# Ending the deferred output projection eleven granules earlier in a streamed-weight attention kernel

## The chip, the cores and the metric

The kernel runs on one core of one Trainium2 chip. The metric is the device time of one execution in microseconds, as the median of several executions. The kernel before takes 1866.62 us (median of 3 runs, 1864.03 to 1872.82).

## The reference

A sequence of 2048 rows of width 1024 is normalised (`xn`) and goes through two branches whose results are added to `x`.

```python
# branch A: 64 segments of 32 rows, one after the other
for s in range(n_seg):
    xs = x[:, s*32:(s+1)*32, :]
    h = concatenate([mem, xs], axis=1)         # 8 memory rows + 32 rows
    q = einsum('btd,dhe->bhte', h, Wq)         # 32 heads of 128
    k = einsum('btd,dhe->bhte', h, Wk)
    v = einsum('btd,dhe->bhte', h, Wv)
    p = softmax(where(mask, q @ k.T * scale, -1e9))
    o = einsum('bhte,hed->btd', p @ v, Wo)
    mem = o[:, :8, :]                          # memory of the next segment
    outs.append(o[:, 8:, :])
# branch B: the 2 best of 2048 rows by x @ w_r go through a gated MLP (1024 -> 3584 -> 1024)
return x + A(xn) + B(xn)
```

The segments depend on one another only through the 8 memory rows. Of the 40 rows of a segment, the first 24 rows of its input together with the 8 memory rows (32 rows) are what the next segment needs. The last 8 input rows of a segment, called the *left* rows here, are not needed by the recurrence. Four segments form a *group*, and the left rows of a group (4 x 8 = 32 rows) go through the weights together, one group ahead for q, k and v and after the group for the output projection.

## The kernel before, in words

**Steps, phases and granules.** There are 64 steps, one a segment; a step `s` is `j = s % 4` of its group. The weights are cut into 64 granules of 128 x 2048 bf16 (512 KB). Granules 0 to 47 are six phases of eight: q first half, k first half, q second half, k second half, v first half, v second half. Granules 48 to 63 are the sixteen pieces of the output projection. A step walks through all 64 in order: `(p, kc)` is granule `8*p + kc`, and `(6, w)` is granule `48 + w`. In each granule TensorE (PE) makes 4 matmuls of 32 x 512 side by side in the array for the 32 main rows (L817), or 8 of 32 x 256 in the output projection (L586).

**Resident and streamed weights.** 44 granules stay on the chip. The other 20 are fetched again in each step (19 after the first step, since granule 6 is kept in PSUM, and half of granule 25 is too) from a scratch copy in HBM (`wsc`) into 5 slots (`g`). The fetches are issued on SyncE's queue (SP, L366), each as soon as the slot that it will fill has been released by the last PE instruction that reads it. Before granule 25 is used, VectorE (DVE) copies its kept half from PSUM into its slot (L393, hooks (2,1) and (2,2)).

**Work hung into the order.** Small pieces of work are hung behind granules: `hook(p, kc, fn)` runs `fn` in the program's order behind granule `8*p + kc`. The engines execute their instructions in that order, each its own list. What matters here:

- behind phase 1 ScalarE (ACT) casts the k sums to `XB` (L836); at (2,3) PE transposes them (L649) and DVE copies them to `KT` (L664), with a small ACT copy of the left rows' k (L662);
- at (2,6) PE makes the scores of the first half, `scores(0)` (L672, L674), into the PSUM tile `BS`; they need the whole of `KT`. DVE then masks and shifts them (L681 to L687);
- at (3,4) ACT takes the exponent (L691) and DVE normalises and transposes (L696 to L720, `soften(0)`);
- at (4,6) PE makes the scores of the second half, `scores(1)`, into the same `BS`, so it waits until `soften(0)` has read it;
- in steps with `j = 0` POOL (GpSimd) loads the next group's left x (L333 into `BX`, hook (1,1)); in every step it loads the next segment's x at (2,4) (L281).

**Passes of the left rows.** `PASSES` says behind which granule of which `j` each left pass is made. A pass is 4 matmuls of 32 x 512 (L579 for q, k, v; L598 for the output projection, `project_left`, into the PSUM tile `WL`). The 16 passes of unit `o` (granules 48 to 63) begin in the step `j = 3` of a group and end in the step `j = 0` that follows. `COPIES` says where a unit's sums are copied out. For `o` this is `copy_unit`: two ACT copies of 64 x 256 (L616) into `LF`, two DVE adds (L619) into `LF`, one POOL add (L620) of `LF` and the scaled left x `OL`, and four DMAs on POOL's queue (L624). `OL` is loaded at the end of the step `j = 3` (L333) and scaled by `sum_left` on DVE (five small instructions, L275 to L347).

The lists at the top of the program (`PASSES`, `COPIES`) and the calls of `hook` set the order by hand; no planner changes it.

Of the kernel before, what the change touches and what calls it, by code (L numbers as in the profile page):

```python
# [43 lines left out]
}  # L44

COPIES = {"q0": (1, 1, 0, "scalar"), "q1": (1, 5, 7, "vector"), "k0": (2, 2, 0, "scalar"), "k1": (2, 5, 7, "vector"),
          "v0": (3, 4, 7, "scalar"), "v1": (3, 5, 7, "scalar"), "o": (0, 3, 3, "vector")}


@with_exitstack  # L50
def kernel(
# [221 lines left out]
    def two_rows(m, tag):  # L273
        t = one.tile([P, 4], F32, tag=tag, name="RI")
        nc.vector.tensor_copy(out=t[:, 0:1], in_=m[:, 0:1])  # L275
        nc.vector.reciprocal(out=t[:, 1:2], in_=m[:, 1:2])
        return t
# [63 lines left out]
    def sum_left(t, G):  # L341

        mr = two_rows(ML[:, G, :], "ri")
        nc.vector.tensor_scalar(out=mr[:, 0:1], in0=mr[:, 0:1], scalar1=mr[:, 1:2], scalar2=-1.0,
                                op0=ALU.mult, op1=ALU.mult)
        nc.vector.tensor_scalar(out=mr[:, 1:2], in0=mr[:, 1:2], scalar1=1.0, scalar2=None, op0=ALU.add)
        nc.vector.tensor_scalar(out=t[:, :], in0=t[:, :], scalar1=mr[:, 1:2], scalar2=mr[:, 0:1],  # L347
                                op0=ALU.mult, op1=ALU.add)
# [241 lines left out]
    xl_of, otl_of = [None], [None]  # L590
# [41 lines left out]
    for s in range(NSEG):  # L632
        G, j = divmod(s, 4)
# [9 lines left out]
        def hook(p, kc, fn):  # L643
            hooks.setdefault((p, kc), []).append(fn)
# [140 lines left out]
                held.pop(g)  # L785
                after(s, g)
        if j == 0 and s > 0:
            hook(2, 3, lambda: sum_left(xl_of[0], G - 1))
        hook(*((1, 0) if s > 0 else (2, 3)), clear_pl)
        if s > 0:  # L790
            hook(0, 0, lambda: bring_back(3, nc.scalar.copy))
# [222 lines left out]
```

## Time and profile before

| | before |
|---|---|
| median of the runs | 1866.62 us |
| the profiled execution, time | 1871.21 us |
| its span, first to last instruction | 1869.1 us |
| mean granted TensorE clock | 0.957 |
| PE busy | 1568.8 us (84%) |
| DVE / ACT / POOL busy | 896.9 / 683.6 / 457.1 us |
| moved by DMA | 712.27 MB, mean 381 GB/s |

Times in the profile are microseconds from the first instruction. PE is a matmul, PEld a weight load (which overlaps matmuls), SPq and POOLq are engines in their role of issuing DMAs. A row of the timeline is: start, duration, engine, line, operation, what it writes and reads, how many instructions are merged in it, and in brackets how long the engine sat idle before it and what ended that. `A <- B: t, n, m` in the list of waits means that instructions A waited `t` us in total for B, `n` times, `m` us at the longest.

### The profile page before, as it was taken

To read this page: it belongs to the slowest core of one execution; us is meant where nothing else is said; L and a number is where in the kernel's file an instruction comes from. 1 tells how busy PE (TensorE), PEld (TensorE's weight loads), DVE (VectorE), ACT (ScalarE), POOL (GpSimd) and SP (SyncE) were. 2 spreads that over 40 slices of the span, in tenths; PEclk is the share of its full clock that TensorE was granted. 3 is DMA by queue.
4 is the path that set the end of the run, shared out by engine and by line. 5 is a ranking of instruction groups with operands and counts; after the bars stand their busy time and mean duration, and the time that the engine had idled before them with its cause. 6 is when DMAs were issued, how large, how long until landed. Compare 5 with 4: busy or idle time off the path is not lost.

```text
span 1869.1 us, 80529 instructions
## 1 busy us (share of the span) xinstructions
PE 1568.8 (84%) x34978; PEld 847.9 (45%) x34978; DVE 896.9 (48%) x2950; ACT 683.6 (37%) x1933; POOL 457.1 (24%) x898
## 2 busy tenths in 40 slices
PE   3458998898998988888899988988889988988764
PEld 1124444444444444444444444444445544444433
DVE  6725544554455444544554455544544455445430
ACT  1113433444343433434344334434334343433320
POOL 3111322213231322223132322323132221312220
PEclk8669999999999999999999999999999999999995
DMA  9999999999999999999999999999999999999998
GB/s 370 406 355 373 388 386 380 393 382 387 394 385 392 366 383 391 359 380 385 388 375 388 389 384 387 373 396 374 378 369 396 394 382 383 378 377 352 384 402 338
DMA packets 230322, 712.27 MB, mean 381 GB/s; under 512 B 39040, under 2 KB 52912, under 8 KB 229968
## 3 DMA queue, kind: packets, MB, share of 16 engines
q1 hardware_dynamic: 192592, 671.18, 93.0%
q0 software_dynamic: 28736, 28.08, 4.7%
q10 hardware_dynamic: 8640, 7.87, 1.2%
q8 instruction: 274, 4.49, 0.9%
q14 instruction: 80, 0.66, 0.1%
HBM read 694.32 MB, written 22.29 MB: 383 GB/s over the span
## 4 chain that ended last, share of the span: by engine, by line
DMA 61%; PE 32%; DVE 4%; issue 1%; ACT 1%; SPq 0%; ACTq 0%; DVEq 0%
DMA g<-wsc 54%; PE PSm L817 17%; PE WO L586 4%; PE PSl L579 4%; PE BT L649 2%; DMA XP<-in_A_x_dram 2%; PE WL L598 1%; DMA MW<-in_B_w_gate_dram 1%; DVE XR L256 1%; DMA MW<-in_B_w_up_dram 1%; DMA g<-in_A_Wq_dram 1%; DMA wres<-in_A_Wo_dram 1%; DMA g<-in_A_Wo_dram 1%; DMA MW<-in_B_w_down_dram 1%; DMA g<-in_B_w_down_dram 1%
## 5 line engine op out<-in xcount | busy, mean ns | idle before, releaser
L817 PE MATMUL PSm<-wres,ST 128*32 128x512 bf16 x8448 | 700.5, 383 | 6.5 <-DMA wres<-in_A_Wv_dram 3.5
L817 PEld LDWEIGHTS <-ST 128*32 128x32 bf16 x12288 | 323.6, 96 | 412.7 <-issue 168.2
L817 PE MATMUL PSm<-g,ST 128*32 128x512 bf16 x3588 | 360.0, 386 | 97.7 <-DMA g<-wsc 76.3
L586 PEld LDWEIGHTS <-OT 128*32 128x32 bf16 x8192 | 217.6, 97 | 166.6 <-issue 141.0
L836 ACT CAST XB<-PSm 128x512 bf16<-128x512 f32 x256 | 150.7, 589 | 283.9 <-PE PSm L817 280.8
L586 PE MATMUL WO<-wres,OT 128*32 128x256 bf16 x5632 | 237.6, 278 | 12.3 <-DMA wres<-in_A_Wo_dram 8.0
L495 POOL DMA_DIRECT2D LX<-ql_d x63 | 35.4, 562 | 814.0 <-PE WO L586 423.2
L586 PE MATMUL WO<-g,OT 128*32 128x256 bf16 x2560 | 133.3, 281 | 84.1 <-DMA g<-wsc 72.6
L579 PE MATMUL PSl<-wres,STL 128*32 128x512 bf16 x2112 | 184.5, 390 | 0.4 <-issue 0.4
L887 POOL DMA_DIRECT2D out_dram<-X x256 | 130.2, 515 | 211.9 <-DVE X L885 169.4
L664 DVE COPY KT<-BT 128x512 bf16<-128x512 bf16 x112 | 45.9, 410 | 278.7 <-issue 121.8
L281 POOL DMA_DIRECT2D X<-in_A_x_dram x256 | 130.1, 515 | 179.6 <-PE PSm L817 88.8
L389 ACT COPY BK<-KEPT 128x512 bf16<-128x512 bf16 x126 | 74.3, 590 | 131.2 <-PE WO L586 99.8
L657 ACT COPY QT<-BT 128x512 bf16<-128x512 bf16 x128 | 75.0, 586 | 127.1 <-PE BT L502 78.1
L649 PEld LDWEIGHTS <-XB 128*128 128x128 bf16 x1024 | 58.6, 98 | 117.1 <-ACT XB L836 75.2
L885 DVE TENSOR_TENSOR X<-WO,X 128x256 bf16<-128x256 f32 x64 | 27.2, 425 | 172.3 <-PE WO L586 172.3
L649 PE MATMUL BT<-IDENT,XB 128*128 128x128 bf16 x1024 | 102.2, 223 | 8.2 <-ACT XB L836 6.7
L579 PEld LDWEIGHTS <-STL 128*32 128x32 bf16 x3072 | 84.0, 98 | 53.0 <-issue 8.5
L846 ACT CAST VM<-PSm 128x512 bf16<-128x512 f32 x128 | 76.5, 598 | 83.3 <-PE PSm L817 82.8
L736 PEld LDWEIGHTS <-VM 32*128 32x128 bf16 x2048 | 65.1, 91 | 83.7 <-issue 72.7
L393 DVE COPY g<-KEPT 128x512 bf16<-128x512 bf16 x126 | 47.6, 420 | 101.7 <-PE PSm L817 51.5
L681 DVE TENSOR_TENSOR BS<-BS,CT 128x96 f32<-128x96 f32 (+1 forms) x256 | 59.1, 231 | 72.8 <-PE BS L674 68.3
(175 smaller groups left out, 2371.9 us busy)
## 6 DMA issues: line engine op xcount, KB each, us to landing
g<-wsc SPq DMA_DIRECT2D x1134, 512.0 KB, 6.0
g<-wsc SPq DMA_DIRECT2D x63, 256.0 KB, 5.7
LX<-ql_d POOLq DMA_DIRECT2D x63, 128.0 KB, 5.6
ql_d<-XBl ACTq DMA_DIRECT2D x60, 128.0 KB, 5.8
MW<-in_B_w_gate_dram SPq DMA_DIRECT2D x16, 448.0 KB, 9.5
MW<-in_B_w_up_dram SPq DMA_DIRECT2D x16, 448.0 KB, 9.1
wres<-in_A_Wk_dram SPq DMA_DIRECT2D x12, 512.0 KB, 11.9
MW<-in_B_w_down_dram SPq DMA_DIRECT2D x12, 512.0 KB, 10.1
```

The source lines that it names most:

```text
L281: nc.gpsimd.dma_start(out=X[s % 2][32 * g:32 * g + XM, :], in_=x2[s * SEG:s * SEG + XM, 256 * g:256 * (g + 1)])
L389: copy(out=back[c][:, :], in_=KEPT_COLS[KEPT_WHOLE][c])
L579: nc.tensor.matmul(PSl[32 * jq:32 * jq + 32, :], lhsT=STL[:, g % KC, :], rhs=part(Gv, jq), start=first_, stop=last_, tile_position=(0, 32 ...
L586: nc.tensor.matmul(PS[32 * g:32 * g + 32, 0:256], lhsT=lhs(h), rhs=Gv[:, D * hs + 256 * g:D * hs + 256 * (g + 1)], start=(first and hs == ...
L649: nc.tensor.transpose(out=PTq[:, il, :, :].rearrange("p j r -> p (j r)"), in_=XB[:, il * P:(il + 1) * P], identity=IDENT[:, :])
L657: nc.scalar.copy(out=QT[half][:, :, :], in_=pv)
L681: nc.vector.tensor_tensor(out=S4, in0=S4, in1=m, op=ALU.add)
L736: nc.tensor.matmul(o, lhsT=VM[half][q0:q0 + 32, il * P:(il + 1) * P], rhs=PTm[q0:q0 + 32, il, 0:NK], start=True, stop=False, tile_position ...
L817: nc.tensor.matmul(PSm[32 * jq:32 * jq + 32, :], lhsT=ST[:, kc, :], rhs=part(Gv, jq), start=(kc == 0), stop=(kc == KC - 1), tile_position= ...
L836: nc.scalar.copy(out=XB[:, :], in_=PSm[:, :])
L846: nc.scalar.copy(out=VM[half][:, :], in_=PSm[:, :])
L887: nc.gpsimd.dma_start(out=out2[s * SEG:s * SEG + XM, 256 * g:256 * (g + 1)], in_=OB[32 * g:32 * g + XM, :])
```

## The change

Three things move, and only in steps with `j = 0` (steps 4, 8, ... 60: fifteen steps):

1. The last six passes of unit `o`. Before, they stood behind granules 7, 11, 15, 19, 22 and 26 of the step. Now they stand behind granules 4, 7, 10, 12, 14 and 16.
2. `copy_unit("o")`, from (3,3) to (2,1): before, behind granule 27; now behind granule 17, one granule after the last pass. All its instructions move, on ACT, DVE, POOL and POOL's DMA queue.
3. `sum_left`, from (2,3) to (1,4).

The number of instructions is the same on every engine, and SyncE's list is unchanged.

```diff
 PASSES["o"]:
-          (3, 8, 0): [52, 54], (0, 0, 7): [55], (0, 1, 3): [57], (0, 1, 7): [58], (0, 2, 3): [60], (0, 2, 6): [61],
-          (0, 3, 2): [63]},
+          (3, 8, 0): [52, 54], (0, 0, 4): [55], (0, 0, 7): [57], (0, 1, 2): [58], (0, 1, 4): [60], (0, 1, 6): [61],
+          (0, 2, 0): [63]},
...
 COPIES:
-          "v0": (3, 4, 7, "scalar"), "v1": (3, 5, 7, "scalar"), "o": (0, 3, 3, "vector")}
+          "v0": (3, 4, 7, "scalar"), "v1": (3, 5, 7, "scalar"), "o": (0, 2, 1, "vector")}
...
         if j == 0 and s > 0:
-            hook(2, 3, lambda: sum_left(xl_of[0], G - 1))
+            hook(1, 4, lambda: sum_left(xl_of[0], G - 1))
```

**DVE, from the start of a `j = 0` step to `soften(0)`.** `L885` and `L324` belong to the step's start, `L347` is the last of `sum_left`, `L619` are the adds of `copy_unit`, `L393` fills granule 25's kept half, `L664` makes `KT`, and `L681` is the first instruction after `scores(0)`. Before:

```order
L389 COPY BK<-KEPT_193 128x512
L393 COPY g<-KEPT_195 128x512 x2
L664 COPY KT<-BT 128x16x32
L275 COPY RI<-BS 128x1
...
L347 TENSOR_SCALAR OL<-OL,RI 128x256
L681 TENSOR_TENSOR BS<-BS,CT 128x4x24
...
L687 TENSOR_TENSOR BS<-BS,NM 128x320
L619 TENSOR_TENSOR LF<-WL,LF 64x256 x2
L696 TENSOR_REDUCE DN<-BS 128x8
```

Now:

```order
L389 COPY BK<-KEPT_193 128x512
L275 COPY RI<-BS 128x1
...
L347 TENSOR_SCALAR OL<-OL,RI 128x256
L619 TENSOR_TENSOR LF<-WL,LF 64x256 x2
L393 COPY g<-KEPT_195 128x512 x2
L664 COPY KT<-BT 128x16x32
L681 TENSOR_TENSOR BS<-BS,CT 128x4x24
...
L687 TENSOR_TENSOR BS<-BS,NM 128x320
L696 TENSOR_REDUCE DN<-BS 128x8
```

(What is left out, the middle of `sum_left` and of the masking, stands in the same order in both.) The two adds stood between `scores(0)` and `soften(0)`; they now stand ahead of the two copies L393 and of `KT`.

**ACT, behind phase 0's `QKL`.** `L836` is the cast behind each phase, `L616` are the copies of `copy_unit`, `L691` is the exponent of the first half.

```order
 L506 COPY QKL<-BT 128x512
 L836 CAST XB<-PSm 128x512
-L662 COPY KT<-QKL 128x16x8
-L836 CAST XB<-PSm 128x512
-L657 COPY QT<-BT 128x512
 L616 COPY LF<-WL 64x256 x2
+L662 COPY KT<-QKL 128x16x8
+L836 CAST XB<-PSm 128x512
+L657 COPY QT<-BT 128x512
 L691 ACTIVATE BS<-BS 128x320
```

The two copies stood just ahead of the exponent; they now follow the cast of phase 1, ahead of the small `KT` copy.

**POOL, in the same step.** `L620` adds `LF` and `OL`, `L624` stores, `L281` loads the next segment's x.

```order
 L763 MEMSET BX 128x256
 L333 DMA BX<-in_A_x_dram 32x1x256 x4
-L281 DMA X_131<-in_A_x_dram 24x256 x4
-L620 TENSOR_TENSOR OL<-LF,OL 128x256
-L624 DMA out_dram<-OL 4x8x256 x4
+L620 TENSOR_TENSOR OL<-LF,OL 128x256
+L624 DMA out_dram<-OL 4x8x256 x4
+L281 DMA X_131<-in_A_x_dram 24x256 x4
```

The add and the stores stood behind the load of x; they now stand ahead of it.

## The prediction

> **What bounds the kernel now.** I read the page first, then the waits and one line's view of the stream, then the timeline of one `j = 0` step.
>
> ```profile
> span 1869.1 us, 80529 instructions
> ...
> DMA  9999999999999999999999999999999999999998
> ...
> HBM read 694.32 MB, written 22.29 MB: 383 GB/s over the span
> ...
> DMA 61%; PE 32%; DVE 4%; issue 1%; ACT 1%; SPq 0%; ACTq 0%; DVEq 0%
> ```
>
> The DMA engines are busy in every slice, and 61% of the chain of waits is transfer. PE is the next link, 32%: each fetch needs a slot that PE has released. So the stream of weights sets the pace, and PE matters where it releases late.
>
> ```profile
> L885 DVE TENSOR_TENSOR X<-WO,X x64: 424/425/427, 129.5 to 1810.4; 128x256 bf16<-128x256 f32 x64
> ...
> g<-wsc SPq DMA_DIRECT2D x1134, 512.0 KB, 6.0
> ...
> DMA to landing us min/median/max: 3.3/6.0/10.3
> ...
> SPq L366 <- PE PSm L817: 422.9, 640, 2.7
> SPq L366 <- DMA g<-wsc: 396.5, 740, 2.5
> ...
> PE PSm L817 <- DMA g<-wsc: 76.3, 154, 2.5
> PE WO L586 <- DMA g<-wsc: 72.6, 150, 2.0
> ```
>
> L885 ends each step: 63 steps in 1680.9 us are 26.7 us a step. A fetch of 512 KB (0.524 MB) at 383 GB/s is 1.37 us of transfer, but lands 6.0 us after its issue in the median and 3.3 us at best. So 2.7 us (about two granules) is waiting behind others: that is the reserve which keeps the DMA engines fed. PE waits for data 76.3 + 72.6 us in all, 2.4 us a step, and SP waits for PE about as long as for transfers.
>
> The step below (`j = 0`, from 528.7 to 554.8) is where the change acts; first PE from the end of phase 1 to `scores(0)`:
>
> ```profile
> 532.46 0.40 PE L817 MATMUL PSm<-g,ST 128*32 128x512 bf16 x4 [0.19 <-DMA g<-wsc]
> ...
> 534.89 0.40 PE L598 MATMUL WL<-wres,OTL 128*32 128x512 bf16 x4
> 535.10 0.40 PE L817 MATMUL PSm<-wres,ST 128*32 128x512 bf16 x4
> 535.52 0.40 PE L817 MATMUL PSm<-g,ST 128*32 128x512 bf16 x4
> ...
> 536.50 0.40 PE L649 MATMUL BT<-IDENT,XB 128*128 128x128 bf16 x4
> 536.83 0.40 PE L817 MATMUL PSm<-wres,ST 128*32 128x512 bf16 x4
> 537.06 0.39 PE L817 MATMUL PSm<-g,ST 128*32 128x512 bf16 x4
> ...
> 537.71 0.19 PE L672 MATMUL BS<-KT,QT 128*32 128x40 bf16 x4
> ```
>
> A pass or a granule takes PE 0.21 us (534.89 to 535.10), the four transposes 0.33. Next, what ACT and DVE do around it, and POOL's rows:
>
> ```profile
> 534.62 0.59 ACT L506 COPY QKL<-BT 128x512 bf16<-128x512 bf16 x1
> 535.12 0.59 ACT L836 CAST XB<-PSm 128x512 bf16<-128x512 f32 x1
> 540.43 0.74 ACT L616 COPY LF<-WL 64x256 f32<-64x256 f32 x2
> 541.09 0.42 ACT L691 ACTIVATE BS<-BS 128x320 f32<-128x320 f32 x1
> ...
> 531.46 0.76 DVE L393 COPY g<-KEPT 128x512 bf16<-128x512 bf16 x2 [1.26 <-DMA g<-wsc]
> 536.99 0.42 DVE L664 COPY KT<-BT 128x512 bf16<-128x512 bf16 x1 [4.78 <-issue]
> 539.65 0.50 DVE L687 TENSOR_TENSOR BS<-BS,NM 128x320 f32<-128x320 f32 x1
> 541.21 0.86 DVE L619 TENSOR_TENSOR LF<-WL,LF 64x256 f32<-64x256 f32 x2 [1.06 <-ACT LF L616]
> 542.10 0.49 DVE L696 TENSOR_REDUCE DN<-BS 128x8 f32<-128x320 f32 x1
> 543.21 0.29 DVE L715 TENSOR_TENSOR BX<-BS,DN 128x64 bf16<-128x64 f32 x1
> 543.55 0.11 PEld L672 LDWEIGHTS <-QT 128*32 128x32 bf16 x3 [0.50 <-DVE BX L715]
> ...
> 542.16 0.67 POOL L620 TENSOR_TENSOR OL<-LF,OL 128x256 bf16<-128x256 f32 x1 [4.65 <-DVE LF L619]
> 543.12 2.44 POOL L624 DMA_DIRECT2D out_dram<-OL  x4 [0.29 <-POOL OL L620]
> ...
> 549.69 0.34 DVE L292 TENSOR_SCALAR XN<-X,RI 128x256 bf16<-128x256 bf16 x1
> ```
>
> Two things to see. DVE had L393 done at 532.2 and then stood idle 4.78 us, free for `KT` as soon as PE had transposed. And `scores(1)` (543.55) waits for `soften(0)`, which the LF copies and adds hold up. The first is lost by the change, the second is won.
>
> **The change, part by part.** All work is kept; what counts is order, in fifteen steps.
>
> *Passes earlier.* Five passes instead of two now stand ahead of the end of phase 1: 3 x 0.21 = 0.64 us later. In this step PE waits for granule 9 (0.19, and the pipeline's own gap beside it), which takes up one pass: +0.43. So `XB`, at 535.12, starts at 535.55. From step to step this is between 0.2 and 0.65.
>
> *The new wait.* The last pass follows one granule later; PE is done with it at 535.55 + 0.43 = 535.98. ACT's next instruction can start 0.50 after `XB` (534.62 to 535.12): LF copies 536.05 to 536.79. DVE's adds 0.04 behind (541.17 to 541.21), 0.86: to 537.69. Then, queued behind them, L393's 0.76 to 538.47 and `KT`'s 0.42 to 538.89. PE's scores come 0.30 behind `KT` (537.41 to 537.71): **539.19 instead of 537.71, 1.5 us later**. Without the wait PE would be there at 535.98 + six granules (1.29) + 0.33 = 537.60. So PE stands idle 1.6 us at (2,6), once in each of the fifteen steps. Behind it on PE wait granules 23, 24 and 25, with them the release of 25's slot, and so the fetch of 42.
>
> *The wait that goes.* From `scores(0)` to `scores(1)` it is now 543.56 - 537.71 = 5.85 us. Without copies and adds: scores to end of L687 2.44, exponent 0.05 + 0.42, then L696 to the end of L715 0.03 + 1.40, PE 0.06: 4.4. PE's own work there is 16 granules and two transpositions, 3.44 + 0.66 = 4.1. So 539.19 + 4.4 = 543.6: by `scores(1)` PE has made good its delay. Those who wait there now:
>
> ```profile
> PEld L672 <- DVE KT L664: 27.9, 68, 0.9
> ...
> PEld L672 <- DVE BX L715: 10.1, 15, 0.7
> ```
>
> The second wait, 0.7 us in each of fifteen steps, goes; the first grows by about 15 x 1.6 = 24 us, with single waits over 0.9 that do not occur now.
>
> *What the idle 1.6 us cost the stream.* This is the term that the trace of before doesn't hold directly. From release of 21 (PE at 537.06) to that of 25 it was 1.3 us; now 2.7 to 2.9. Granules 29 and 33 follow late by some 1.3 and 1 us. From below: nothing, if 1.6 us fits into the reserve of 2.7. From above: the whole 1.6, 24 us in all. The nearest rows are in another step, where SP issued nothing from 1278.6 to 1281.9:
>
> ```profile
> L366 SPq DMA_DIRECT2D g<-wsc x2: 319/320/320, 1278.6 to 1281.9; - x2
> ...
> 1281.00:1282.00 1.00, 0.57 (x12) 0.35 (x15) 0.00 (x0) 0.00 (x0) 0.54 (x2) 1.00 1.07 423
> 1282.00:1283.00 1.00, 1.00 (x28) 0.50 (x20) 0.00 (x0) 0.59 (x1) 1.00 (x3) 1.00 1.12 302
> 1283.00:1284.00 1.00, 1.00 (x20) 0.46 (x16) 0.01 (x1) 0.01 (x1) 1.00 (x3) 1.00 0.70 162
> ```
>
> (Columns: window, us, busy time and count of PE, PEld, DVE, ACT, POOL, then clock, DMA share, GB/s.) The rate held for the gap and fell behind it, by 121 and 261 GB/s in one microsecond each: 382 KB, 0.9 us of the stream at 423. Our gap is shorter, but the fetch before it comes 0.2 to 0.4 us late already (the passes), and two more late ones follow. I take 0.85 us a step, nearest to that row: 15 x 0.85 = **+13 us**. It can't be won back later in the step, since the rest is limited by transfers.
>
> *Nothing else.* `sum_left` runs in DVE's idle stretch; its loads (issued at the end of the step before) must land by the adds at 536.8, otherwise they would delay `KT` too. POOL's add and stores now end about 3.1 us behind the adds, at 540.8, and the load of x behind them (2.1 us of issuing, some 5 to land) by 548: `L292` needs it at 549.69. This cover is 1.7 us; if it were gone, DVE would hold up the attention copies behind L292.
>
> The sum for the profiled execution: 1871.2 (span 1869.1 and 2.1 around it) + 13 = 1884. It lay 4.6 above the median of the runs; so the median goes from 1866.6 to **1879.6**, 0.7% slower.
>
> **The rivals.**
>
> *The reserve takes it.* 2.7 us of reserve against 1.6: the stream never runs dry, PE arrives on time at `scores(1)`, and each of the fifteen steps costs at most 0.2 us: 1866.6 + 0 to 3 = 1868. For it: the two numbers. Against it: the gap of 3.3 us above, which cost 0.9 with the same reserve, and that two fetches are late, not one. The Trainium skill, DMA: Bandwidth & Descriptors, Anatomy of one DMA, gives a single DMA (measured there on GpSimd's path) about 2.0 us plus its bytes at 436 GB/s; for 0.524 MB that is an estimate of 3.2 us, and the trace's best landing of 3.3 agrees; by that rule a delay of 1.6 us out of 6.0 would be hidden, and the sum would be this rival's.
>
> *The removed wait decides (faster).* If PE's delay at `scores(0)` were smaller than reckoned, because granules up to 25 are late themselves and PE would have stood there anyway, what is left is the shorter way to `scores(1)`: 0.7 to 0.87 us a step, PE being the pace: 15 x 0.8 = 12, 1855. It decides once the data for granules 17 to 25 come over 1.2 us later than PE needs them. Against it: in this step PE waits for none of these.
>
> *The whole delay arrives.* The stream runs dry and PE's 1.6 us is lost in full: 24 us, 1891. For it: SP issues are bound to PE's releases for half of its waiting. Against it: PE's waits of 2.4 us a step for data, which would shrink first.
>
> *The change does not do what it says*: no; the lists show the adds ahead of `KT`.
>
> **How the numbers follow.** Forecast (1872 to 1886) 0.50, reserve 0.28, whole delay 0.11, faster 0.11. This kernel's measurement can't tell under 0.5% (9.3 us) from no change. The forecast lies above that bound in about nine tenths (0.45); with the whole delay, slower is 0.56. Same takes the rest of the forecast and most of the reserve: 0.33. Faster 0.11. The range leaves out the ends of both outer cases: 1863 to 1893; the likeliest case's own range is 1872 to 1886.
>
> **What would show it.** Right: the wait of L672 for `KT` at 45 us or more in total, singles of 1.2 to 1.9; that for L715 gone; from `scores(0)` to `scores(1)` 4.4 to 4.8 instead of 5.85; the moved GB/s lower for about 2 us behind (2,6) in `j = 0` steps; these steps 0.5 to 1.2 us longer, the others unchanged. Wrong: `KT` not late, or late while the `j = 0` steps keep their length (then the reserve was enough).

## The result, and the profile after

The changed kernel takes 1889.83 us (median of 6 runs, 1884.49 to 1891.42); the kernel before, beside it, 1865.32 us (median of 6, 1861.63 to 1872.88). The ratio is **1.0125, 95% interval 1.0101 to 1.0149**: the change makes the kernel slower by 24.5 us, 1.6 us for each of the fifteen steps that it touches. The forecast was slower, 1879.6 us with a range to 1893: the direction and the place were right, the loss in a step was forecast at about half its size. (Counted in granules, the last pass moved from behind 26 to behind 16 and the copy from behind 27 to behind 17: ten granules, not the eleven of the title.)

The page of the changed kernel:

```profile
span 1889.7 us, 80567 instructions
...
HBM read 694.32 MB, written 22.29 MB: 379 GB/s over the span
...
DMA 58%; PE 36%; DVE 3%; issue 1%; SPq 1%; ACT 0%; DVEq 0%; ACTq 0%
...
L885 DVE TENSOR_TENSOR X<-WO,X x64: 423/425/426, 129.9 to 1832.7; 128x256 bf16<-128x256 f32 x64
```

The same bytes move at 379 in place of 383 GB/s, and PE's share of the chain has grown from 32 to 36%. (PE, DVE, ACT and POOL have as many busy instructions as before; the 38 more in the first line are not among them.) From the first to the last L885 it is 1702.8 us in place of 1680.9. Taken apart by the starts of that line, the `j = 0` steps have grown from 27.15 to 28.63 us in the mean; the others are as before (26.64 and 26.62 for `j = 1`, 26.82 and 26.73, 26.15 and 26.25). Fifteen times 1.48 us are 22.2 us, the whole of the 21.9 by which these two stretches differ.

The waits of the first scores, in the list of waits; one row of before:

```profile
PE BS L672 <- DVE KT L664: 2.6, 11, 0.4
```

Now:

```profile
PEld L672 <- DVE KT L664: 55.6, 88, 1.8
PE BS L672 <- DVE KT L664: 22.0, 24, 1.3
...
PE BS L672 <- ACT KT L664: 2.5, 15, 0.2
```

The rows `PE BS` are the idle time of the matmul side, from the end of the last matmul. For the first `KT` it was 2.6 us in all before and is 22.0 now: 1.3 us more in each `j = 0` step. The rows for `soften(0)` (10.1 us on PEld and 2.9 on PE, for L715) are gone; on PE another of about the same length stands in their place, 2.5 us for the second `KT`, a copy on ACT.

One `j = 0` step of the changed kernel, the same one as shown of before, from 535.0 to 563.2; PE, then ACT and DVE in the timeline:

```profile
544.46 0.39 PE L817 MATMUL PSm<-wres,ST 128*32 128x512 bf16 x4
546.14 0.21 PE L672 MATMUL BS<-KT,QT 128*32 128x40 bf16 x4 [1.29 <-DVE KT L664]
...
542.72 0.59 ACT L836 CAST XB<-PSm 128x512 bf16<-128x512 f32 x1 [0.92 <-PE PSm L817]
543.33 0.74 ACT L616 COPY LF<-WL 64x256 f32<-64x256 f32 x2
...
542.00 0.35 DVE L347 TENSOR_SCALAR OL<-OL,RI 128x256 bf16<-128x256 bf16 x1 [4.99 <-DMA out_dram<-X]
544.11 0.86 DVE L619 TENSOR_TENSOR LF<-WL,LF 64x256 f32<-64x256 f32 x2 [1.77 <-PE BT L649]
545.00 0.75 DVE L393 COPY g<-KEPT 128x512 bf16<-128x512 bf16 x2
545.67 0.41 DVE L664 COPY KT<-BT 128x512 bf16<-128x512 bf16 x1
```

This is the queue that the prediction wrote down: cast, LF copies, adds, L393, `KT`, scores, with nothing between them, and PE standing still for 1.29 us. `sum_left` waited for its loads until 542.00, 2.1 us ahead of the adds; that cover held. (This row names a store on the same queue; in 13 of the 15 steps the releaser named is the load of `OL`, and in all of them `sum_left` ends 1.7 us or more ahead of the adds.)

What the stream did meanwhile, in windows of two microseconds (window, us, busy time and count of PE, PEld, DVE, ACT and POOL, clock, DMA share, GB/s):

```profile
534.99:563.17 28.18, 22.91 (x525) 12.39 (x519) 13.99 (x50) 11.35 (x32) 10.35 (x20) 1.00 0.98 361
542.00:544.00 2.00, 2.00 (x38) 0.95 (x26) 0.34 (x1) 1.24 (x3) 1.25 (x3) 1.00 0.96 319
544.00:546.00 2.00, 0.85 (x14) 0.23 (x12) 1.84 (x5) 0.38 (x2) 0.66 (x1) 1.00 0.95 334
546.00:548.00 2.00, 1.86 (x60) 1.14 (x64) 1.30 (x5) 0.59 (x1) 1.99 (x4) 1.00 0.97 389
548.00:550.00 2.00, 2.00 (x36) 0.90 (x36) 1.42 (x4) 1.50 (x3) 2.00 (x5) 1.00 0.88 287
550.00:552.00 2.00, 1.84 (x59) 0.94 (x57) 1.51 (x6) 0.98 (x3) 0.48 (x1) 1.00 0.84 264
552.00:554.00 2.00, 1.27 (x32) 0.60 (x28) 1.41 (x5) 0.93 (x4) 0.00 (x0) 1.00 1.06 348
```

And the whole step and the corresponding stretch of before:

```profile
528.75:554.83 26.08, 23.04 (x526) 12.48 (x522) 13.95 (x50) 11.19 (x33) 10.60 (x20) 1.00 1.03 395
538.00:540.00 2.00, 2.00 (x48) 1.09 (x41) 1.81 (x6) 0.75 (x2) 0.00 (x0) 1.00 1.02 386
540.00:542.00 2.00, 1.59 (x32) 0.57 (x24) 0.93 (x3) 1.95 (x5) 0.00 (x0) 1.00 1.02 388
542.00:544.00 2.00, 1.84 (x56) 0.90 (x56) 1.87 (x7) 0.90 (x3) 1.55 (x3) 1.00 1.03 408
```

PE stands still in the window 544 to 546, but the rate is lowest two to six microseconds later, at 287 and 264 GB/s, while PE is busy again. This one step was already slow ahead of the gap (319), so the mean of the fifteen steps is the better witness. Counted from the start of the first scores, the rate from 2 us ahead to 2 us behind is the same in both kernels (351 GB/s now, 354 before); from 2 to 8 us behind it is 307 against 385, 0.47 MB less. In the step shown, the mean of the ten microseconds from 544 is 324 GB/s, against some 395 before: 71 x 10 = 0.71 MB less, 1.8 us of the stream at 395. The step is 2.1 us longer.

### The profile page after: what moved, and what is told of

It is laid out like the page before. It is cut to its first block, busy times and chain, and to the rows that moved or that the text cites. A ratio compares the mean times of both kernels' runs of the same rounds, so it can differ in the third digit from the quotient of the medians.

```text
span 1889.7 us, 80567 instructions
## 1 busy us (share of the span) xinstructions
PE 1573.0 (83%) x34978; PEld 852.7 (45%) x34978; DVE 898.1 (48%) x2950; ACT 686.1 (36%) x1933; POOL 455.8 (24%) x898
## 4 chain that ended last, share of the span: by engine, by line
DMA 58%; PE 36%; DVE 3%; issue 1%; SPq 1%; ACT 0%; DVEq 0%; ACTq 0%
DMA g<-wsc 52%; PE PSm L817 19%; PE WO L586 5%; PE PSl L579 4%; PE BT L649 2%; DMA XP<-in_A_x_dram 2%; PE WL L598 1%; DMA MW<-in_B_w_up_dram 1%; DMA MW<-in_B_w_gate_dram 1%; DVE XR L256 1%; DMA g<-in_A_Wq_dram 1%; DMA wres<-in_A_Wo_dram 1%; PE BT L301 1%; PE BS L672 1%; DVE g L393 1%
## 5 line engine op out<-in xcount | busy, mean ns | idle before, releaser
L817 PE MATMUL PSm<-g,ST 128*32 128x512 bf16 x3588 | 361.0, 386 | 104.2 <-DMA g<-wsc 82.7
L586 PEld LDWEIGHTS <-OT 128*32 128x32 bf16 x8192 | 221.5, 99 | 167.0 <-issue 139.2
L836 ACT CAST XB<-PSm 128x512 bf16<-128x512 f32 x256 | 150.5, 588 | 314.1 <-PE PSm L817 311.2
L586 PE MATMUL WO<-wres,OT 128*32 128x256 bf16 x5632 | 242.8, 284 | 11.5 <-DMA wres<-in_A_Wo_dram 8.2
L586 PE MATMUL WO<-g,OT 128*32 128x256 bf16 x2560 | 135.5, 287 | 86.5 <-DMA g<-wsc 76.8
L281 POOL DMA_DIRECT2D X<-in_A_x_dram x256 | 130.4, 514 | 172.1 <-PE PSm L817 66.4
L664 DVE COPY KT<-BT 128x512 bf16<-128x512 bf16 x112 | 45.7, 408 | 202.4 <-ACT XB L836 93.3
L885 DVE TENSOR_TENSOR X<-WO,X 128x256 bf16<-128x256 f32 x64 | 27.2, 425 | 166.6 <-PE WO L586 166.6
L681 DVE TENSOR_TENSOR BS<-BS,CT 128x96 f32<-128x96 f32 (+1 forms) x256 | 59.7, 233 | 87.4 <-PE BS L674 83.0
L745 DVE CAST OT<-BT 128x128 bf16<-128x128 f32 x128 | 37.3, 291 | 132.2 <-PE BT L301 74.2
```

Of the source, the lines that this page charges most:

```text
L281: nc.gpsimd.dma_start(out=X[s % 2][32 * g:32 * g + XM, :], in_=x2[s * SEG:s * SEG + XM, 256 * g:256 * (g + 1)])
L586: nc.tensor.matmul(PS[32 * g:32 * g + 32, 0:256], lhsT=lhs(h), rhs=Gv[:, D * hs + 256 * g:D * hs + 256 * (g + 1)], start=(first and hs == ...
L681: nc.vector.tensor_tensor(out=S4, in0=S4, in1=m, op=ALU.add)
L817: nc.tensor.matmul(PSm[32 * jq:32 * jq + 32, :], lhsT=ST[:, kc, :], rhs=part(Gv, jq), start=(kc == 0), stop=(kc == KC - 1), tile_position= ...
L836: nc.scalar.copy(out=XB[:, :], in_=PSm[:, :])
```

## The experiments

Each kernel was timed against the kernel before on the same chip; the differences below are ratio times the median of before (1868.7 to 1870.4 us), and "idle" is PE's own wait for `KT` (rows `PE BS <- DVE`) beyond the 2.6 us of before, divided by fifteen steps. "Idle" counts from the end of the last matmul, which the profile puts 0.4 us behind its start, although the next granule can start after 0.21; so PE's real delay is up to 0.2 us longer (a table in the next section has it). The theory: `KT` behind the adds makes PE stand still at the first scores, the slots are released late, and the stream loses what it can't make up. The rivals: the earlier passes themselves (B), POOL's new order of stores and loads (C), and a reserve that takes short delays.

### Only the passes moved

```diff
-  "o": (0, 2, 1, "vector")        # of the change
+  "o": (0, 3, 3, "vector")        # as before
-  hook(1, 4, lambda: sum_left(xl_of[0], G - 1))
+  hook(2, 3, lambda: sum_left(xl_of[0], G - 1))
```

> The six passes stand where the change puts them; the copies and sum_left stay where they were, so KT is not behind the adds. Theory A (the late KT makes PE stand still about 1.3 us at the first scores, the stream runs dry, and that is the loss): no wait of L672 for KT beyond that of the kernel before (27.9 us in all), 0 to +4 us against the kernel before. Theory B (the earlier passes themselves, which release granules 13 to 21 up to 0.6 us later, cost the time): +15 to +24 us.

Measured: 1867.72 us, ratio 0.9998 (0.9975 to 1.0021). The idle row is `PE BS L672 <- DVE KT L664: 3.1, 7, 1.5` in place of 2.6. The passes cost nothing, and they do not delay the releases either: the fetches of granules 29 to 39, which wait for the slots of 9 to 21, are issued at most 0.12 us later than before in the mean of the `j = 0` steps. B falls.

### The sums copied two granules later

```diff
-  "o": (0, 2, 1, "vector")
+  "o": (0, 2, 3, "vector")
```

At (2,3) the transposes and `KT` come first, the LF copies and adds behind them; POOL's order and everything else are those of the change.

> The change with one difference: the left sums are copied behind the transposes of (2,3), two granules later, so on DVE KT stands ahead of the two adds. Passes, sum_left and POOL's order (add and stores ahead of the load of x) are those of the change. A: KT is not late, from -8 to +4 us against the kernel before (a gain if the shorter way from the first to the second scores is worth anything). B, or theory C (POOL's stores and loads in their new order slow the stream): +15 to +24 us, as the change.

Measured: 1871.01 us, ratio 1.0036 (1.0007 to 1.0064), +6.7 us. Two granules of difference in where the copy is written win back some 18 of the 24.5 us, with POOL's order unchanged: C falls as the main cause. The waits of the first scores are close to those of before:

```profile
PEld L672 <- DVE KT L664: 31.7, 78, 2.0
PE BS L672 <- DVE KT L664: 3.9, 8, 1.5
```

The expectation ended at +4. What the remaining few microseconds come from was not tried, and POOL's order (C) could be part of them; the lower end of the interval is near zero.

### The wait alone, in the kernel before

```diff
+ for _ in range(5 if j == 0 and s > 0 and not half else 1):
      (nc.scalar.copy if j == 0 and half else nc.vector.tensor_copy)(out=KT[half][:, :, 0:32], in_=pv)
```

> The kernel before with one difference: in steps with j = 0 DVE makes the first KT copy five times in place of once, 4 x 0.34 = 1.4 us more ahead of the first scores. Passes, copies, POOL as before. A: PE idle at L672 for KT grows by about 15 x 1.4 = 21 us and the time by +15 to +26 us. Reserve theory (1.4 us fits into the 2.7 us that a fetch waits behind others): 0 to +4 us. B and C: 0.

Measured: 1896.28 us, ratio **1.0148** (1.0112 to 1.0184), +28 us. Nothing else differs from the kernel before (`sum_left`, behind the copies on DVE, comes later with them; `soften(0)` ends no later after the first scores, 5.79 for 5.83 us), and the loss of the change is there. In the list of waits (lines have moved by one; the wait is credited to `RI`, the instruction just behind the copies on DVE):

```profile
PE BS L673 <- DVE RI L276: 21.8, 15, 1.6
...
PE BS L673 <- DVE KT L665: 2.3, 4, 1.0
```

Idle 1.4 us a step, loss 1.8 us a step. The reserve theory, 0 to +4, falls.

### L393 ahead of the adds

```diff
-  hook(2, 1, lambda: kept_piece(KEPT_PART, 2, nc.vector.tensor_copy))
-  hook(2, 2, lambda: kept_piece(KEPT_PART, 3, nc.vector.tensor_copy))
+  hook(*((1, 1) if j == 0 else (2, 1)), lambda: kept_piece(KEPT_PART, 2, nc.vector.tensor_copy))
+  hook(*((1, 2) if j == 0 else (2, 2)), lambda: kept_piece(KEPT_PART, 3, nc.vector.tensor_copy))
```

> The change with one difference: in steps with j = 0 the two copies of granule 25's kept half (L393) are made at (1,1) and (1,2), so only the adds and not these 0.76 us stand ahead of KT. PE's idle at the first scores falls from about 1.3 to about 0.5 us a step. A with a loss in proportion to the idle: +8 to +11 us against the kernel before. A with a threshold (a short idle fits into the reserve): 0 to +4. B or C: +15 to +24.

Measured: 1879.63 us, ratio 1.0054 (1.0025 to 1.0083), +10 us.

```profile
PEld L672 <- DVE KT L664: 40.2, 82, 1.1
PE BS L672 <- DVE KT L664: 9.3, 20, 0.6
```

Idle 0.45 us a step, loss 0.7. Taking 0.76 us of DVE work out of the queue ahead of `KT` returned 14.5 us, about 1 us a step. The loss shrinks with the idle time, and no idle time short enough to be free was seen.

### Half the dose

Three `KT` copies in place of one, else as the run with five.

```diff
+ for _ in range(3 if j == 0 and s > 0 and not half else 1):
```

> The late first KT of a j = 0 step with half the dose: three copies in place of one, 0.7 us more, all else as before. In proportion to the idle time: +12 to +14 us. With a threshold below which the reserve takes it: 0 to +5 us.

Measured: 1888.47 us, ratio 1.0093 (1.0059 to 1.0128), +17 us (11 to 24). Idle 0.6 us a step (rows for `RI` and `KT`), loss 1.2 (0.7 to 1.6). No threshold here either.

### The same wait in another step

Five `KT` copies for the first half in steps with `j = 1` (fifteen steps).

```diff
+ for _ in range(5 if j == 1 and s > 1 and not half else 1):
```

> The kernel before with one difference: in steps with j = 1 (5 to 61) DVE makes the first KT copy five times in place of once: the wait of the run with the late first KT, at the same place of another step, which has no output passes and no left copies. If a j = 0 step is nothing special: +15 to +28 us, as that run's +28. If the loss came from what else a j = 0 step holds: under +8 us.

Measured: 1884.42 us, ratio 1.0082 (1.0054 to 1.0110), +15 us.

```profile
PE BS L673 <- DVE KT L665: 23.7, 23, 1.8
```

Idle 1.4 us a step as in the `j = 0` run, but loss 1.0 in place of 1.8 us; the intervals (10 to 21 us, and 21 to 34) just do not overlap. So such a loss does not need a `j = 0` step, but a `j = 0` step loses more.

### The same wait later in the step

Five `KT` copies for the second half in steps with `j = 1`, ahead of the second scores.

```diff
+ for _ in range(5 if j == 1 and s > 1 and half else 1):
```

> The kernel before with one difference: in steps with j = 1 (5 to 61, fifteen steps) DVE makes the second KT copy (behind (4,3), ahead of the second scores) five times in place of once, 1.4 us more. The same wait as in the run with the late first KT, but some 5 us later in the step, where more of the stream is in flight (2.7 granules by issues and bytes, against 1.8 to 2.0 at the first scores of a j = 0 step). Reserve theory (what is in flight at the place decides): +3 to +14 us. Every idle microsecond of PE counts in full: +18 to +26 us.

Measured: 1887.15 us, ratio 1.0095 (1.0060 to 1.0130), +18 us (11 to 24).

```profile
PE BS L673 <- DVE KT L665: 25.7, 21, 1.8
```

Idle 1.5 us a step, loss 1.2. It lies at the edge between the two expectations. What is in flight when the wait begins (bytes issued on SyncE's queue less bytes moved, mean of the fifteen steps) is 3.0 granules here, 2.7 in the run with the late first `KT` in `j = 1`, and 2.5 in that with the late first `KT` in `j = 0`, not the 1.8 to 2.0 of the expectation. These counts lie close together and the intervals of the losses are wide: the run does not show that what is in flight decides, nor that it doesn't.

### The sums copied behind `soften(0)`

```diff
-  "o": (0, 3, 3, "vector")        # of the kernel before
+  "o": (0, 3, 5, "vector")
```

> The kernel before with one difference: the left sums are copied at (3,5) in place of (3,3), so behind soften(0) on ACT and DVE. From the first to the second scores the way falls from 5.85 to about 4.5 us, and PE's wait of 0.7 to 0.87 us a step for soften(0) goes. If PE's standing still costs the same wherever it is: -10 to -13 us against the kernel before. If it costs only where it starves the stream (here more than two granules are in flight): -3 to +2 us.

Measured: 1871.35 us, ratio 0.9996 (0.9970 to 1.0022). Both rows for `BX L715` (10.1 us on PEld, 2.9 on PE) have gone from the list of waits. But PE's wait has not gone. Its row before:

```profile
PE BS L672 <- DVE BX L715: 2.9, 13, 0.2
```

And in this run:

```profile
PE BS L672 <- ACT KT L664: 2.3, 14, 0.2
```

The second scores need the second `KT` too, an ACT copy in `j = 0` steps, and that one stands behind the LF copies in both kernels. ACT in the `j = 0` step shown of before:

```profile
541.53 0.59 ACT L836 CAST XB<-PSm 128x512 bf16<-128x512 f32 x1
542.86 0.58 ACT L664 COPY KT<-BT 128x512 bf16<-128x512 bf16 x1
```

And in one of this run, with PE's second scores:

```profile
544.03 0.43 ACT L691 ACTIVATE BS<-BS 128x320 f32<-128x320 f32 x1
544.49 0.74 ACT L616 COPY LF<-WL 64x256 f32<-64x256 f32 x2
545.26 0.58 ACT L836 CAST XB<-PSm 128x512 bf16<-128x512 f32 x1
546.59 0.58 ACT L664 COPY KT<-BT 128x512 bf16<-128x512 bf16 x1
547.22 0.21 PE L672 MATMUL BS<-KT,QT 128*32 128x40 bf16 x4 [0.16 <-ACT KT L664]
```

Before, the LF copies stand ahead of the exponent and the cast of phase 3 right behind it; here they stand between the two. In the mean of the `j = 0` steps `soften(0)` ends 4.50 us after the first scores in place of 5.83, but the second `KT` ends at 5.78 in both, and the second scores start at 5.83 in place of 5.89. So the edit shortened PE's way by 0.06 us, not by the 1.3 that was expected, and the equal time says nothing of what a shorter way would be worth.

### The late `KT`, with the sums copied behind `soften(0)`

The late first `KT` in `j = 0` steps, and the sums copied at (3,5), which was meant to free PE's way from the first to the second scores.

```diff
-  "o": (0, 3, 3, "vector")        # of the kernel before
+  "o": (0, 3, 5, "vector")
+ for _ in range(5 if j == 0 and s > 0 and not half else 1):
```

> The late first KT of a j = 0 step (five copies in place of one, as in the run that took 28 us more), with the left sums copied at (3,5), behind soften(0). A late KT of the same length cost 28 us in j = 0 steps and 15 us in j = 1 steps. If the difference is that a late PE cannot make good its delay in a j = 0 step, since soften(0) stands behind the LF copies there: about +15 us against the kernel before. If it is that less of the stream is in flight there: +23 to +28 us.

Measured: 1894.85 us, ratio 1.0143 (1.0102 to 1.0184), +27 us. Idle 1.55 us a step, loss 1.8. The way was not freed, for the reason of the run before: it takes 5.81 us here and 5.85 in the run with the late `KT` alone. So this run repeats that loss, and why a `j = 0` step loses more stays open.

### The passes early, the copy behind `soften(0)`

```diff
-  "o": (0, 2, 1, "vector")        # of the change
+  "o": (0, 3, 5, "vector")
```

> The change with one difference: the left sums are copied at (3,5), behind soften(0), so neither KT nor soften(0) stands behind the adds. Passes early, sum_left at (1,4). If the removed wait at the second scores is worth something: -10 to -13 us against the kernel before, and the best of all. If not: -3 to +2 us. More would mean that the early passes or sum_left cost something after all.

Measured: 1864.55 us, ratio **0.9972** (0.9949 to 0.9996), -5 us. The idle row is `PE BS L672 <- DVE KT L664: 3.7, 12, 0.6`. The passes of the change can stay where the change puts them, if the sums are copied where nobody waits behind the copies. It is the best of all, but by less than the 0.5% under which the prediction counts a time as unchanged. Here too the second `KT` ends 5.54 us after the first scores, `soften(0)` at 4.27, so PE's way is only 0.3 us shorter than before, with one pass gone from it, and the wait at the second scores is not removed in this run either.

## Why the prediction was right or wrong

**The bound.** Right: the stream sets the pace, and a slot that is released late is paid for. One reading of the waits was wrong, though. "SP waits for PE about as long as for transfers" takes the largest row alone; with the other three rows of L366 for PE (213.6, 138.6 and 48.1 us beside the 422.9) SyncE waits 823 us for PE's releases and 397 for transfers. PE's releases were about twice the share that the text gave them.

**Passes earlier.** They were reckoned at +0.43 us on PE's way to the first scores. In the mean of the fifteen steps PE could have begun these scores 0.17 us later than before in the changed kernel, and no later in the run with the passes alone, which cost nothing.

**The new wait.** Right in its place and its chain, and a little too long. Counted as the prediction did, from when PE could have issued the scores, the delay is 1.45 us in the mean and 1.47 in the step shown, in place of 1.6; the 1.29 of the row is shorter only because it counts from the end of the last matmul. The link that was mis-sized is the last one. The 0.30 us from the end of `KT` to the scores in the kernel before were mostly PE's own work there; where PE stands waiting, the scores follow the end of `KT` (545.67 + 0.41 = 546.08) by 0.06 us, at 546.14.

**The wait that goes.** Half right. From the first to the second scores it is 4.9 us (546.14 to 551.08) in place of 5.85; forecast were 4.4. The sum left out the second `KT`, on ACT behind the LF copies and the cast of phase 3. In the kernel before it ended only 0.05 us ahead of `soften(0)` in the mean, so a faster `soften(0)` would have gained next to nothing by itself. The change shortens the way all the same, since it takes the LF copies from ahead of that cast too (it starts 2.87 us after the first scores in place of 3.85); with the copies put back behind the exponent and the passes left early, the way is 5.6 us again. Granule 42 is reached only 0.4 us later in the mean (17.35 for 16.93 us after the step's start), where granule 25 was 1.6 late: PE has nearly made good its delay there, as forecast. Then it waits for data (0.7 us at granule 45, 0.1 before) and is 1.5 us late again at granule 62. The delay left PE and came back as missing bytes.

**What the idle time cost the stream.** This is the term that failed: "I take 0.85 us a step, nearest to that row", and measured are 1.6. The row was cut off too early. It took the two slow microseconds behind the gap; the four that follow were slow too:

```profile
1284.00:1285.00 1.00, 1.00 (x52) 0.61 (x48) 0.92 (x5) 0.29 (x1) 0.59 (x2) 1.00 0.91 353
1285.00:1286.00 1.00, 1.00 (x32) 0.59 (x25) 0.88 (x4) 0.59 (x1) 0.00 (x0) 1.00 0.99 316
1286.00:1287.00 1.00, 1.00 (x20) 0.43 (x16) 0.93 (x3) 0.17 (x1) 0.00 (x0) 1.00 0.94 344
1287.00:1288.00 1.00, 1.00 (x28) 0.46 (x23) 0.15 (x1) 0.98 (x3) 0.00 (x0) 1.00 0.97 356
```

By the prediction's own working (what is missing against 423 GB/s) these add 70, 107, 79 and 67 KB to the 382: 705 KB, 1.7 us in place of 0.9. That is one gap, and a longer one, so it is no proof; but read to its end the row would have given about what was measured. In the changed kernel, too, the rate is low for about six microseconds. Counted from the step's start, the fetch of 42 is issued 1.6 us later than before, and those of 45, 47 and 50 by 1.4, 1.2 and 0.7; the text named the first two of these ("two more late ones follow") but priced them at nothing. The two bounds were right, and the result lies at the upper one, "the whole 1.6, 24 us in all". That the measured time lies inside the stated range is owed to the upper rival, for which the range was kept open, and not to this term.

How a delay and its loss went together, in microseconds a step. The delay is how much later the scores start behind the granule ahead of them than in the kernel before, mean of the fifteen steps of the profiled execution; the loss is from the runs.

| | delay of PE | loss (95%) |
|---|---|---|
| the change | 1.45 | 1.6 (1.3 to 1.9) |
| the wait alone | 1.62 | 1.8 (1.4 to 2.3) |
| the same, sums copied at (3,5) | 1.73 | 1.8 (1.3 to 2.3) |
| half the dose | 0.79 | 1.2 (0.7 to 1.6) |
| L393 ahead of the adds | 0.68 | 0.7 (0.3 to 1.0) |
| `j = 1`, first scores | 1.51 | 1.0 (0.7 to 1.4) |
| `j = 1`, second scores | 1.57 | 1.2 (0.7 to 1.6) |

In each run on `j = 0` steps the delay lies inside the interval of the loss: it is paid in full, as far as these runs can tell.

**The reserve rival.** For 0.524 MB the Trainium skill, DMA: Bandwidth & Descriptors, Anatomy of one DMA, gives about 3.2 us (2.0 plus bytes at 436 GB/s, fitted there on GpSimd's path; an estimate). The best landing agrees, 3.3 us before and 3.5 after. But the conclusion that the other 2.7 of the median 6.0 us are spare does not hold here: delays of 0.7 to 0.8 us already cost 0.7 and 1.2 us a step.

**The other rivals.** Faster: its condition did not come about, since in the changed kernel's `j = 0` steps PE waits for none of the granules 17 to 25 and was held 1.45 us by `KT`. What a shorter way to the second scores is worth by itself no run shows. Its price of 0.7 to 0.87 us a step came mostly from PEld's row; the matmul side's own row (2.9 us in all) has 0.2 a step. The whole delay arrives: 1891 us, with a chance of 0.11, came nearest to the 1889.83 measured. Its reason against, "PE's waits of 2.4 us a step for data, which would shrink first", did not come true: these waits grew from 148.9 to 159.5 us in all (82.7 and 76.8 now).

**The signs.** The wait of L672 for `KT` is 55.6 us (45 or more forecast) with singles up to 1.8, the wait for L715 is gone, the rate is lower behind (2,6), the `j = 0` steps are longer and no others: all came. The steps were to be 0.5 to 1.2 us longer and are 1.48, the rate was to be lower for about 2 us and is so for about 6, and 4.9 us from first to second scores lies just over the 4.4 to 4.8.

## What to carry to other kernels

Where a stream is refilled slot by slot as its reader releases, look for what stands ahead, in each engine's own list, of the small result that the reader waits for next: here two adds that nobody was in a hurry for, put two granules too early, cost most of 1.3%. Before pricing a wait that an edit removes, look for what else the waiting instruction needs: here a second result ended 0.05 us ahead of the one that the trace named, and two runs built to remove the wait removed nothing. Read a slow stretch to its end before taking a price from it. And do not take the difference between the usual and the best landing time for a reserve: price a late release at its full length until a run shows less.

## What the runs showed of the hardware

The rate of the transfers falls after the gap, not in it. In the mean of the fifteen steps it is 351 GB/s from 2 us ahead of the late scores to 2 us behind them, as before (354), and 307 from 2 to 8 us behind, against 385; in the step shown the DMA share fell from 0.96 (544 to 548) to 0.86 (548 to 552). A gap of 1.45 us on PE thus shows as about six slow microseconds in the moved bytes. And in `j = 0` steps the loss was about as long as PE's delay, 1.6 us for 1.45, 1.8 for 1.62, 0.7 for 0.68; in `j = 1` steps it was 1.0 for 1.51 and 1.2 for 1.57, though the second interval (0.7 to 1.6) still takes in the whole delay. What makes the difference between the two kinds of steps was not found.
